# Gated mix of a cached attention and a gated MLP, one token: weights loaded once for several matmuls, the gated unit in rows, and projections added up in two banks

## The chip, the cores and the metric

The kernel runs on one NeuronCore of one Trainium2 chip. A core has a matrix engine (TensorE, PE in the profile; its weight loads are PEld), a vector engine (VectorE, DVE), an activation engine (ScalarE, ACT), GpSimd (POOL) and a queue engine (SyncE, SP) that here issues all large transfers. On-chip memory is SBUF (128 partitions) and PSUM (8 banks of 128 x 512 fp32 into which TensorE writes). Data comes from HBM through 16 DMA engines. The metric is the device time in microseconds (us). The kernel before takes 386.67 us, the median of 7 runs (386.39 to 387.09).

## What is computed

One token `x` of 1024 numbers goes through an attention block A and a mixer block B, mixed by a scalar gate:

```python
g = sigmoid((x * gate_w).sum())
# A: 32 query heads, 4 key/value heads, 65536 cached positions, head size 128
q = x @ wq                                 # 1024 -> 32 x 128
p = softmax(q k^T / sqrt(128));  o = p v   # 8 query heads share one k, v
a = o.reshape(4096) @ wo                   # 4096 -> 1024
# B: F = 3584, Fh = 1792, sequence of one
z = gelu(x_b @ w_in)                       # 1024 -> 3584
z1, z2 = z[:Fh], layernorm(z[Fh:])
b = (z1 * (w_sp * z2 + b_sp)) @ w_out      # 1792 -> 1024
out = g * a + (1 - g) * b
```

In the kernel both blocks read the same `x`. All inputs are bf16. K and V are 64 MiB each, and with the weights 162 MB are read for 2 KB of output.

## The kernel before

Every operation is recorded by `P(engine, function, r=..., w=...)` in program order. A planner derives the waits from what each operation reads and writes; each engine then executes its own operations strictly in the recorded order. So the order in the source is the order on each engine, and whatever is recorded behind a waiting operation on the same engine waits as well.

All large loads go through SyncE into a ring of five slots (`NS = 5`) of 4 MB. The stream is a fixed list: two loads of wq, then K pairs (8192 positions a piece, two pieces a load) mixed with two loads of w_in and one of w_out, then K and V pairs in turn, then wo in pieces. Load n takes the slot of load n - 5, and is issued when the last operation that reads that slot has been recorded as done (`done`, `issue`). Counted from 0, the first loads are: 0 and 1 wq, 2 K 0,1, 3 w_in, 4 K 2,3, 5 w_in, 6 K 4,5, 7 w_out, 8 K 6,7, 9 K 8,9, 10 V 0,1, 11 K 10,11, 12 V 2,3, 13 K 12,13. Load 12 so takes the slot of w_out, and load 11 that of K 4,5.

Query projection (L414 to L442): for each of 8 chunks of x, eight matmuls of 512 columns, spread over four column groups of the array (`tile_position=(0, 32 * cg)`), all into one bank; then a cast, transposes and a selection bring q into a padded form.

K pieces (`k_piece`, L456): a piece is worked in four batches. VectorE transposes 128 x 1024 32-bit words (L464), TensorE runs four matmuls of 512 columns with a weight load each (L472), into one of two score banks; two bank numbers alternate by piece. `score_piece` copies a finished bank to SBUF and takes its maximum. Exponentials lag by one head group (8 pieces); `pt_piece` transposes them and `pv_piece` (L510) multiplies them with V in four column groups (L516). `out_piece` closes a head group: sum, reciprocal, scale, selection, and a column vector `ovec`.

Mixer: `win_piece` (L552) makes the 3584 numbers of z as columns: 28 columns of 128 values, each from matmuls with a moving operand of one column (L558, 224 in all). `mixer_piece` (L566) computes gelu, layernorm and gate on tiles of 128 x 28 and leaves `yb`. `wout_piece` (L599) multiplies by w_out with four column groups of 256 columns (L606) into one bank, which ScalarE copies to `brow`. These pieces are recorded behind K pieces 1, 3 and 6, before the first V arrives.

The end: for each wo load, matmuls of 256 columns in four column groups add into one bank (L650); VectorE adds `brow` (L656) and SyncE writes the output.

## Time and profile before

| what | value |
|---|---|
| time, median of 7 runs | 386.67 us (386.39 to 387.09) |
| the profiled execution | 386.39 us, span in the profile 384.6 us |
| TensorE busy | 230.1 us (60%), 1547 matmuls and 1547 weight loads |
| VectorE busy | 211.7 us (55%) |
| ScalarE busy | 30.6 us (8%) |
| DMA | 162.24 MB, mean 422 GB/s |
| mean granted TensorE clock | 0.798 |

The page divides the span into 40 slices; a digit is a busy share in tenths. A row of a timeline or of the groups names start and length, the engine, the source line (L464 is line 464 of the kernel before), the operation, the tiles it writes and reads, their shape, and in brackets how long the engine had been idle and what ended the idle time. `SPq` rows are the transfers that SyncE issues. The tensor names are only `arena` (all of SBUF), `pb` (the PSUM banks) and the inputs. A row of a stretch ends with the granted TensorE clock, the share of the DMA engines that is busy, and GB/s.

### The profile page before, as it was taken

The page shows a single profiled execution, that of the slowest core. Times are in us where ns is not written, and L with a number is a line of the kernel's source. Part 1 is how long each engine was busy: PE and PEld are TensorE (multiplying, and loading weights), DVE is VectorE, ACT ScalarE, POOL GpSimd, SP SyncE. Part 2 cuts the span into 40 slices and gives each one's busy share as a digit, 9 for nine tenths or more (in the row PEclk, how much of TensorE's full clock was granted, in tenths as well). Part 3 has the DMA queues.
Part 4 walks back from the last instruction along what each step waited for, and adds up shares of the span by engine and source line. Part 5 has one row for each costly group of instructions (what it writes and reads, how often), then busy time and mean ns, then how long its engine had stood idle before and what let it go on. Part 6 is the DMA issues. An engine that isn't in the chain of part 4 may idle for free.

```text
span 384.6 us, 3607 instructions
## 1 busy us (share of the span) xinstructions
PE 230.1 (60%) x1547; PEld 85.0 (22%) x1547; DVE 211.7 (55%) x329; ACT 30.6 (8%) x71; POOL 2.1 (1%) x9
## 2 busy tenths in 40 slices
PE   0444888578766656573686484726873939543334
PEld 0111544523211111121222121212220202211121
DVE  4116464399967474655695656645964748511010
ACT  1000000100300000001010000000100000320000
POOL 2000000000000000000000000000000000000000
PEclk9999959579996969595889596968895869755665
DMA  8999999999999999999999999999999999999994
GB/s 328 436 436 440 431 424 444 422 432 429 428 436 429 421 433 436 433 434 431 433 433 424 433 429 429 429 431 437 429 431 429 436 427 429 428 433 436 409 426 177
DMA packets 6228, 162.24 MB, mean 422 GB/s; under 512 B 700, under 2 KB 708, under 8 KB 964
## 3 DMA queue, kind: packets, MB, share of 16 engines
q1 hardware_dynamic: 6200, 162.01, 98.2%
q8 instruction: 12, 0.20, 0.2%
q14 instruction: 4, 0.03, 0.0%
q10 hardware_dynamic: 12, 0.00, 0.0%
HBM read 162.01 MB, written 0.00 MB: 421 GB/s over the span
## 4 chain that ended last, share of the span: by engine, by line
DMA 72%; PE 15%; DVE 12%; issue 0%; SPq 0%
DMA arena<-in_A_k_cache_dram 59%; PE pb L472 10%; DMA arena<-in_A_v_cache_dram 10%; DVE arena L464 9%; DMA arena<-in_A_wo_dram 3%; PE pb L516 2%; PE pb L558 2%; DVE arena L485 1%; DVE arena L507 0%; PE pb L650 0%; DVE arena L533 0%; PE pb L538 0%; SPq L349 0%; PE pb L528 0%; PE pb L495 0%
## 5 line engine op out<-in xcount | busy, mean ns | idle before, releaser
L472 PE MATMUL pb<-arena 128*128 128x512 bf16 x512 | 156.9, 448 | 96.0 <-DVE arena L464 93.9
L464 DVE STREAM_TRANSPOSE arena<-arena 128x1024 f32<-128x1024 f32 x128 | 151.6, 1217 | 77.3 <-DMA arena<-in_A_k_cache_dram 76.7
L472 PEld LDWEIGHTS pb<-arena 128*128 128x128 bf16 x512 | 45.8, 107 | 202.1 <-DVE arena L464 148.3
L516 PE MATMUL pb<-arena 128*32 128x512 bf16 x512 | 39.3, 442 | 20.4 <-DMA arena<-in_A_v_cache_dram 17.9
L502 ACT ACTIVATE arena<-arena 128x512 bf16<-128x512 f32 x32 | 23.0, 720 | 224.0 <-DVE arena L507 171.2
L507 DVE STREAM_TRANSPOSE arena<-arena 128x512 bf16<-128x512 bf16 x32 | 21.7, 679 | 18.2 <-PE pb L516 18.2
L485 DVE TENSOR_SCALAR_CACHE_REDUCE arena<-pb 128x512 f32<-128x512 f32 x32 | 21.5, 672 | 6.6 <-PE pb L472 6.4
L516 PEld LDWEIGHTS pb<-arena 128*32 128x32 bf16 x512 | 12.8, 106 | 44.3 <-issue 36.2
L558 PEld LDWEIGHTS pb<-arena 128*128 128x128 bf16 x224 | 13.8, 159 | 0.4
L558 PE MATMUL pb<-arena 128*128 128x1 bf16 x224 | 13.7, 198 | 0.0
L650 PE MATMUL pb<-arena 128*1 128x256 bf16 x128 | 7.0, 375 | 7.6 <-DMA arena<-in_A_wo_dram 7.5
L530 DVE RECIPROCAL arena<-pb 128x1 f32<-128x1 f32 x4 | 0.7, 168 | 17.0 <-PE pb L528 17.0
L419 PE MATMUL pb<-arena 128*2 128x512 bf16 x64 | 7.2, 627 | 4.3 <-DMA arena<-in_A_wq_dram 4.3
L656 DVE TENSOR_TENSOR arena<-pb,arena 97x256 bf16<-97x256 f32 x1 | 0.4, 425 | 13.8 <-PE pb L650 13.8
L426 DVE CAST arena<-pb 98x512 bf16<-98x512 f32 x1 | 0.7, 691 | 10.7 <-PE pb L419 10.7
L396 PE MATMUL pb<-arena 1*128 1x2 bf16 x1 | 0.2, 159 | 10.3 <-DMA arena<-in_B_b_sp_dram 10.3
L502 ACT ACTIVATION_READ_ACCUMULATOR arena<-arena 128x1 f32 x32 | 6.0, 186 | 0.0
L650 PEld LDWEIGHTS pb<-arena 128*1 128x1 bf16 x128 | 3.1, 101 | 11.1 <-DMA arena<-in_A_wo_dram 8.7
L538 PE MATMUL pb<-arena 128*128 128x128 bf16 x16 | 1.8, 243 | 5.2 <-DVE arena L533 5.2
L573 ACT ACTIVATE arena<-arena 128x28 f32<-128x28 f32 x1 | 0.2, 227 | 57.0 <-DVE arena L572 57.0
L569 DVE COPY arena<-pb 128x28 f32<-128x28 f32 x1 | 0.2, 188 | 7.8 <-PE pb L558 7.8
L398 DVE COPY arena<-pb 128x2 f32<-128x2 f32 x1 | 0.2, 159 | 7.4 <-PE pb L396 7.4
(88 smaller groups left out, 50.4 us busy)
## 6 DMA issues: line engine op xcount, KB each, us to landing
arena<-in_A_k_cache_dram SPq DMA_DIRECT2D x16, 4096.0 KB, 30.9
arena<-in_A_v_cache_dram SPq DMA_DIRECT2D x16, 4096.0 KB, 36.1
arena<-in_A_wq_dram SPq DMA_DIRECT2D x2, 4096.0 KB, 17.0
arena<-in_B_w_in_dram SPq DMA_DIRECT2D x2, 3584.0 KB, 40.8
arena<-in_A_wo_dram SPq DMA_DIRECT2D x3, 2048.0 KB, 34.5
arena<-in_B_w_out_dram SPq DMA_DIRECT2D x1, 3584.0 KB, 35.0
arena<-in_A_wo_dram SPq DMA_DIRECT2D x1, 1024.0 KB, 23.3
arena<-in_A_wo_dram SPq DMA_DIRECT2D x2, 512.0 KB, 13.8
```

The costliest lines, as they stand in the source:

```text
L419: ins = e.matmul(pf(OB)[32 * cg:32 * cg + 2, :], xw[:, 3 * c + 1 - s:3 * c + 3 - s], sl[:, WQ_N * k + 512 * (4 * s + cg):WQ_N * k + 512 * ...
L426: P("DVE", lambda e: e.tensor_copy(qsb[0:98, :], pf(OB)[0:98, :]), w=[("psb", 0), B(OB)])
L464: P("DVE", lambda e: e.transpose(ktb(i).bitcast(F32), sl[:, 2048 * j:2048 * (j + 1)].bitcast(F32)), r=[key], w=[("kt", i % NKTS)])
L472: ins = e.matmul(pf(sb), qpad[g % 2][:, o:o + 128], vw(ktb(i), 64 * f2 + ev, [[128, 16], [2, 32]]), start=(j == 0 and fe == 0), stop=(j == ...
L485: P("DVE", lambda e: e.tensor_scalar(scs(n), pf(sb), 0.0, None, op0=ALU.add, op1=ALU.max, accum_out=maxc[:, n:n + 1]), w=[("sc", n % NSC), ...
L502: P("ACT", lambda e: e.activation(psb(n), scs(n), ACTF.Exp, bias=gcol(g, K_NB), scale=SCALE, accum_out=lp[:, n:n + 1]), r=[("sc", n % NSC) ...
L507: P("DVE", lambda e: e.transpose(ptsb(n), psb(n)), r=[("psb", n % 2)], w=[("ptsb", n % 2)])
L516: ins = e.matmul(pf(OB)[32 * cg:32 * (cg + 1), :], ptsb(n)[:, 32 * b:32 * (b + 1)], vw(sl, 128 * b, [[2048, 4], [1, 128]]), start=(u == 0 ...
L530: P("DVE", lambda e: e.reciprocal(gcol(g, K_RL), pf(MB)[:, 0:1]), w=[("rl", g), B(MB)])
L538: ins = e.matmul(pf(MB)[:, 0:128], sel[:, 128 * c:128 * (c + 1)], osc[:, 128 * c:128 * (c + 1)], start=(c == 0), stop=(c == 3))
L558: ins = e.matmul(pf(MB)[:, z:z + 1], vw(sl, c0, [[FC, 128]]), xT[:, 2 * i + k:2 * i + k + 1], start=(i == 0 and k == 0 and z == 0), stop=( ...
L650: ins = e.matmul(pf(FB)[32 * q:32 * q + 1, 0:QW], ovec[:, 8 * i + c:8 * i + c + 1], sl[:, o:o + QW], start=(i == 0 and c == 0), stop=(i == ...
```

## The change

Six parts:

- A matmul can be recorded without a weight load (`again`): it uses the weights of the matmul before it. K pieces are worked in pairs: two transposes, then for each of four weights two matmuls into two banks. There are four score banks (1 to 4), four transposed buffers (`NKTS = 4`) and eight score buffers (`NSC = 8`). Both scores of a pair are copied after the first batch of the next pair.
- The query projection uses one column of x as weights for four matmuls into four banks, in two column groups instead of four (`times`), followed by four casts and eight transposes.
- w_in is done the same way, with 448 columns a matmul, so that z lies in rows: 4 partitions (0, 32, 64, 96) of 896 values. The elementwise work of the gated unit runs on 97 x 896 or 97 x 448 instead of 128 x 28 or 128 x 14; the square moves to ScalarE. 14 transposes and eight small copies make `yb`.
- w_out and the first three wo loads are multiplied as rows of 512 columns, two matmuls per weight, without column groups, and add up in banks 0 and 5. Four copies (`keep`) bring the sum to `brow`.
- The first wo load is worked before the last head group's `out_piece`, since `ovec` of the first group is long there.
- The last wo load (three pieces) keeps its form and has its own bank.

The list of loads and their order stay. The program has 1318 matmuls instead of 1536, and 390 of them load no weights.

## Prediction, made before the changed kernel had run

> **What bounds the kernel now.** I read the page first, then SyncE's own queue, the chain of waits, the timelines of TensorE and VectorE around the gated unit, and last the stretches at the end.

> The page: the transfers fill the span.

> ```profile
> span 384.6 us, 3607 instructions
> ...
> DMA  8999999999999999999999999999999999999994
> GB/s 328 436 436 440 431 424 444 422 432 429 428 436 429 421 433 436 433 434 431 433 433 424 433 429 429 429 431 437 429 431 429 436 427 429 428 433 436 409 426 177
> ...
> q1 hardware_dynamic: 6200, 162.01, 98.2%
> q8 instruction: 12, 0.20, 0.2%
> ```

> Only the first and last slices fall short. The change moves no byte of data, so its time can differ in three ways: the transfers run dry, the work behind the last byte changes, or the small share that is not data (12 instruction packets) changes. How far from dry is it? SyncE issues a 4 MB load when a ring slot comes free:

> ```profile
> 71.27 0.33 SPq L349 DMA_DIRECT2D arena<-in_A_v_cache_dram  x1
> 88.22 0.33 SPq L349 DMA_DIRECT2D arena<-in_A_k_cache_dram  x1
> 96.31 0.33 SPq L349 DMA_DIRECT2D arena<-in_A_v_cache_dram  x1
> 98.81 0.33 SPq L349 DMA_DIRECT2D arena<-in_A_k_cache_dram  x1
> ```

> The chain of waits tells when the last of these landed, and so when each had its turn:

> ```profile
> 98.81 38.46 DMA arena<-in_A_k_cache_dram
> ...
> 137.30 1.25 DVE arena L464
> ```

> 137.27 and the chain's next K landing (176.17, four loads later) give 9.73 us a load. Counting from 0, the load issued at 88.22 is load 11, the one at 96.31 load 12. Load 13 lands at 137.27, so load 12's turn begins at 117.8 and load 11's at 108.1 on the latest of the 16 DMA engines, about 2.1 us earlier on the foremost (the engines' own landing marks: 115.7 to 117.8). From issue to the first byte it takes about 2 us: the first three loads (29.1 us) were issued from 0.73 on and the third landed at 32.5, less 0.6 us between engines. So load 12 may be issued at 113.7 at the latest without loss, 17.4 us after 96.31, and load 11 at 104.0, 15.8 us after 88.22. That is all the cover there is. Load 12 waits for the slot of w_out, that is, for the w_out matmuls, which wait for the gated unit.

> TensorE and VectorE there:

> ```profile
> 14.92 3.58 PE L419 MATMUL pb<-arena 128*2 128x512 bf16 x32
> ...
> 64.41 6.83 PE L558 MATMUL pb<-arena 128*128 128x1 bf16 x112
> ...
> 89.59 1.04 PE L472 MATMUL pb<-arena 128*128 128x512 bf16 x4 [0.30 <-DVE arena L464]
> ```

> ```profile
> 71.27 0.19 DVE L569 COPY arena<-pb 128x28 f32<-128x28 f32 x1 [7.81 <-PE pb L558]
> ...
> 72.63 0.33 DVE L575 RECIPROCAL arena<-arena 128x28 f32<-128x28 f32 x1
> ...
> 76.01 0.16 DVE L588 RECIPROCAL arena<-arena 128x1 f32<-128x1 f32 x1 [0.27 <-ACT arena L587]
> ...
> 77.39 1.24 DVE L464 STREAM_TRANSPOSE arena<-arena 128x1024 f32<-128x1024 f32 x1
> ```

> The first row is 32 matmuls in 8 rounds of four column groups, 0.43 us a round: half clock. The K row is four matmuls 0.218 us apart at full clock, each with its own weight load, whose 98 ns are hidden. The gated unit holds VectorE for 6.12 us (71.27 to 77.39), with the K transposes queued behind it.

> The end:

> ```profile
> 376.51 1.87 PE L650 MATMUL pb<-arena 128*1 128x256 bf16 x32 [3.02 <-DMA arena<-in_A_wo_dram]
> ...
> 378.00:379.00 1.00, 0.38 (x8) 0.00 (x0) 0.00 (x0) 0.00 (x0) 0.00 (x0) 0.50 0.59 242
> 379.00:380.00 1.00, 0.93 (x16) 0.41 (x16) 0.00 (x0) 0.00 (x0) 0.00 (x0) 0.50 0.50 193
> 380.00:381.00 1.00, 0.69 (x12) 0.10 (x8) 0.00 (x0) 0.00 (x0) 0.00 (x0) 0.50 0.22 90
> 381.00:382.00 1.00, 0.53 (x8) 0.10 (x8) 0.00 (x0) 0.00 (x0) 0.00 (x0) 0.50 0.00 0
> ```

> The DMA share (second number from the right) falls in steps: the engines finish between 378.3 and 381.4. They drift apart because an instruction packet occupies one engine for about 1.03 us (0.2% of 16 x 384.6, over 12), and some have served two. TensorE does its 32 matmuls of a w_o load in 1.9 us at half clock and idles 3 us.

> **The change part by part.**

> *Weight reuse in K.* 256 of 512 weight loads go. The K row says they were hidden: 0 us. [...]

> *Query projection.* 16 rounds become 64 matmuls of 512 columns, in runs of four on one column group. If the last of a run overlaps the first of the next group, that is 48 rounds, if not 64. From 14.92, some 5 us at half clock (the K run at 33.84 changed after 4 us), the rest at 0.218: done at 28 to 31, before 26.5. Four casts at 0.69 (one before) and the 2.2 us from cast to first transpose: K starts at 33 to 36 instead of 32.5.

> *K pair, w_in.* Eight transposes at 1.16 plus the last matmuls: K done 46 to 50. Each w_in load is 32 matmuls of 448 columns, 0.191 each, 24 or 32 deep: 4.6 to 6.1 us in place of 6.83. K 2,3 lands at 51.8 as before; 9.3 of transposes, 1.3 of scores, 1.8 of matmuls end at 64.2, w_in at 69 to 70.3. The gated unit so begins 1 to 2 us earlier than 71.27.

> *Gated unit in rows.* The same steps run on 97 x 896 instead of 128 x 28. From the nearest rows: four PSUM copies of 448 (0.69 for 512) 2.5; Square and Exp on ScalarE (0.72 for 512) 1.2 each; two tensor_scalars 0.62 each if they go like the f32 cast (0.43 for 512), 1.1 if not; two tensor_tensors (0.67 for 512) 1.1 each. The reciprocal: 0.328 for 28 and 0.164 for 1 give 6.07 ns an element, 5.6 us for 896, the largest item; its bounds are 1.1 (the rate of the other operations) and 10.5 (0.328/28 with no fixed part), and I take the slope because it alone holds for both rows. Reductions, subtract, square, scale on 448 columns 0.4 to 0.6 each, 3.2 together; the two mean/variance hops as before 2.8; 14 transposes 1.4, eight copies at 0.18 1.45. With handoffs 23.4 us, 6.1 before; bounds 18.9 and 29.3, from those of the reciprocal and the tensor_scalars. [...]

> VectorE returns to K 4,5 at 69.7 + 23.4 = 93.1 instead of 77.39. It was 10.8 us from there to load 11's issue, plus about 1 where TensorE restarts cold: 105, limit 104.0 on the foremost engine and 106.1 on the last: no loss that counts. Then the first half of K 6,7 (4.65 + 1.3 + 1.8) to 113, and w_out.

> *w_out and w_o.* w_out was 14 rounds of 256, 1.7 us; now 28 matmuls of 512 in series at 0.218, 6.1 us, 12 at half clock; I take 6.5. Load 12 is issued at 119.5 to 120, limit 113.7. It flows from 121.7. A foremost engine stood ready at 115.7 and needed 262.6 us from there (378.3); all now restart together, and four later instruction packets instead of seven cost 1.2 on the latest: 121.7 + 262.6 + 1.2 = 385.5, against 381.4. **+4.1.**

> *Fewer instructions.* TensorE goes from 3094 matmuls and weight loads to 2268, at 258 to a packet 8 or 9 packets for 12. Without a stall this alone takes one packet off the latest engine, -1.0; here it is in the 1.2.

> *Tail.* Three w_o loads become 16 matmuls of 512 each in series: 3.5 us at full, 6.8 at half clock, against 4.9 between landings. The first stands ahead of the last head group's output chain (2.0 us). Counting back from the landings, full clock from the first on ends at -0.2; half clock throughout would add 9, but every dense run of 512-column matmuls longer than 5.2 us ended at full clock in this trace, which leaves up to +2.7. The four new copies (about 0.38 each, from 0.29 for 128 columns and 0.42 for the final 256-column add) finish 1.7 after the third load, just about with the last piece. I take +0.3.

> Sum: 386.39 (the profiled execution, span 384.6 and 1.8 around it) + 4.1 + 0.3 = 390.8; the median of the runs shown is 0.28 above that execution: **391.1**.

> **Rivals.**

> *The cover is enough.* If the unit takes under 18 us or the matmuls overlap more, w_out is done by 114 and nothing runs dry. For it: the small rows say little of the rate at 896 columns. Against it: it takes 6 us off my sum. Then 386.67 - 1.0 + 0.3 = 386.0, 385.4 to 387.2: the other side. Decides at issue of load 12 before about 114.

> *Twice starved.* Column groups in series, a reciprocal nearer its upper bound, half clock at each restart: load 11 is late too, w_out ends near 125 and 121.7 grows to 127: 396, 394 to 398. For it: each piece follows idle time of TensorE, and it was at half clock from 70 to 80.

> *The w_o chain at half clock.* It loses the 2.7 of the bound instead of 0.3 where the granted clock falls back before the second load: 393.5 with the stall, 388.4 without.

> *No weight is spared on the path* is no rival but the base: the K part counts nothing in any case.

> **How the numbers follow.** Starved once, as summed, 0.60: 388.0 to 394. Cover enough, 0.15. Twice starved, 0.16. Clock in the tail, 0.09. A measurement here tells about 0.2%, 0.77 us. Of the 0.15, 0.07 lies under 385.9 and 0.08 within the bound; the rest is slower, 0.85. The range leaves out about a tenth on each side: 386.8 to 395.3.

> **What would show it.** VectorE's stretch from the PSUM copies to the next K transpose: 23 us, with a reciprocal of 5.6. Load 12 issued near 119.5, a dip of 3 to 5 us in the GB/s slices near 120, none after. 8 or 9 instruction packets. K matmuls still 0.218 apart. The last w_o landing near 385.5 and about 3.2 us behind it. I am wrong if no slice dips, if the dip is twice as deep, or if the time past the last landing grows.

## The result and the profile after

| | before | changed |
|---|---|---|
| time, median | 386.65 us (39 runs, 386.38 to 387.09) | 388.4 us (16 runs, 385.93 to 390.15) |
| the profiled execution | 386.39 us, span 384.6 | 388.5 us, span 386.6 |

The changed kernel is slower: ratio 1.0044, 95% interval 1.0036 to 1.0053. That is 1.75 us, where 4.4 were forecast. The direction and the mechanism of the prediction hold; the size is off by more than a factor of two.

The page of the changed kernel, with the same lines as before: the span, the share of the DMA engines and the GB/s in 40 slices of 9.67 us, and the queues.

```profile
span 386.6 us, 2806 instructions
...
DMA  8999999999999999999999999999999999999993
GB/s 326 434 434 441 426 431 433 434 434 434 434 388 386 434 434 432 434 434 428 432 424 431 434 434 432 434 434 428 434 432 431 434 428 432 431 432 424 415 422 152
...
q1 hardware_dynamic: 6200, 162.01, 97.8%
q8 instruction: 9, 0.15, 0.2%
```

Two slices dip, 388 and 386, on either side of 116 us. Against 432 they lack 90 GB/s together, which is 2.0 us of full flow (90 x 9.67 / 432). The forecast was a dip of 3 to 5 us near 120. Nothing else dips. The row of digits does not show it at all. The busy share is still 9 tenths there.

SyncE's queue (start, length, source line, what is loaded) shows the loads around the dip; in their order they are load 11, 12 and 13:

```profile
101.54 0.33 SPq L358 DMA_DIRECT2D arena<-in_A_k_cache_dram  x1
115.38 0.33 SPq L358 DMA_DIRECT2D arena<-in_A_v_cache_dram  x1
115.75 0.43 SPq L358 DMA_DIRECT2D arena<-in_A_k_cache_dram  x1
```

Load 12 is issued at 115.38, 1.7 us past the limit of 113.7 that the prediction worked out, but 4.4 us sooner than the 119.5 to 120 it forecast. The timeline of VectorE (start, length, operation, shape, in brackets the idle time before and what ended it) shows where those 4.4 us were gained:

```profile
32.59 4.62 DVE L484 STREAM_TRANSPOSE arena<-arena 128x1024 f32<-128x1024 f32 x4 [0.54 <-DMA arena<-in_A_k_cache_dram]
...
51.98 2.37 DVE L484 STREAM_TRANSPOSE arena<-arena 128x1024 f32<-128x1024 f32 x2 [8.37 <-DMA arena<-in_A_k_cache_dram]
...
67.58 2.51 DVE L589 COPY arena<-pb 33x448 f32<-33x448 f32 x4 [5.21 <-PE pb L248]
...
74.53 5.75 DVE L597 RECIPROCAL arena<-arena 97x896 f32<-97x896 f32 x1
...
89.34 0.95 DVE L632 COPY arena<-pb 32x7 bf16<-32x7 bf16 x8 [1.45 <-PE pb L626]
90.30 2.37 DVE L484 STREAM_TRANSPOSE arena<-arena 128x1024 f32<-128x1024 f32 x2
```

K starts at 32.59, as before. The gated unit runs from 67.58 (the first PSUM copy) to 90.30 (the next K transpose), 22.72 us with a reciprocal of 5.75. Its start, not its length, is what came out well ahead of the forecast (69.7). TensorE's timeline says why, with a stretch of the query projection and one of w_in:

```profile
22.91 0.39 PE L429 MATMUL pb<-arena 128*1 128x512 bf16 x2 [1.86 <-DMA arena<-in_A_wq_dram]
23.12 0.82 PE L248 MATMUL pb<-arena 128*1 128x512 bf16 x6
23.77 0.39 PE L429 MATMUL pb<-arena 128*1 128x512 bf16 x2
...
64.26 0.36 PE L429 MATMUL pb<-arena 128*1 128x448 bf16 x2
64.45 0.74 PE L248 MATMUL pb<-arena 128*1 128x448 bf16 x6
65.02 0.36 PE L429 MATMUL pb<-arena 128*1 128x448 bf16 x2
```

L429 is the matmul with a weight load, L248 the one without (in `again`). Each group counts two of the first and six of the second: one run on each column group. The next two start 0.86 us later (512 columns) and 0.76 us later (448). Eight matmuls so pass in the time of four: K's matmuls of 512 columns start 0.218 us apart, four of them in 0.87. The program issues four on one column group and then four on the other, and still both runs go side by side.

The end of the span. First the stretches of 1 us (length, busy time and count of PE, weight loads, DVE, ACT, POOL; then the granted clock, the DMA share and GB/s), then the timeline:

```profile
380.00:381.00 1.00, 1.00 (x6) 0.17 (x2) 0.00 (x0) 0.00 (x0) 0.00 (x0) 1.00 0.53 217
381.00:382.00 1.00, 1.00 (x16) 0.29 (x12) 0.00 (x0) 0.00 (x0) 0.00 (x0) 1.00 0.20 74
382.00:383.00 1.00, 1.00 (x24) 0.53 (x26) 0.60 (x2) 0.00 (x0) 0.00 (x0) 1.00 0.02 8
```

```profile
381.97 1.38 PE L704 MATMUL pb<-arena 128*1 128x256 bf16 x26
382.38 1.70 DVE L655 COPY arena<-pb 1x256 f32<-1x256 f32 x4 [6.29 <-PE pb L248]
384.12 0.42 DVE L710 TENSOR_TENSOR arena<-pb,arena 97x256 bf16<-97x256 f32 x1
```

Each of the 16 DMA engines marks in the trace when its part of a load has landed. These landing marks put the end of the last load at 379.8 on the foremost engine and at 382.9 on the latest; before it was 378.3 and 381.4. So +1.5 us on both. The final add starts at 384.12, 1.2 us behind the last landing (before 0.7: 382.12 behind 381.4). TensorE ends at 383.35; the four copies end at 384.08, and the add waits for them. Together 1.5 + 0.5 = 2.0 us, which is the whole difference of the spans.

### The profile page after: what moved, and what is told of

The parts are those of the page before. It is cut to its first block, busy times and chain, and to the rows that moved or that the text cites. A ratio compares the mean times of both kernels' runs of the same rounds, so it can differ in the third digit from the quotient of the medians.

```text
span 386.6 us, 2806 instructions
## 1 busy us (share of the span) xinstructions
PE 230.8 (60%) x1329; PEld 53.7 (14%) x939; DVE 230.6 (60%) x350; ACT 31.8 (8%) x71; POOL 3.8 (1%) x11
## 3 DMA queue, kind: packets, MB, share of 16 engines
q1 hardware_dynamic: 6200, 162.01, 97.8%
HBM read 162.01 MB, written 0.00 MB: 419 GB/s over the span
## 4 chain that ended last, share of the span: by engine, by line
DMA 49%; DVE 28%; PE 21%; issue 1%; ACT 1%; SPq 0%; DVEq 0%
DMA arena<-in_A_k_cache_dram 40%; DVE arena L484 17%; DMA arena<-in_A_wo_dram 9%; PE pb L248 8%; PE pb L494 6%; DVE arena L507 3%; PE pb L641 2%; PE pb L538 2%; DVE arena L529 2%; DVE arena L597 1%; DVE arena L589 1%; SPq L358 0%; DVE arena L557 0%; DVE arena L655 0%; PE pb L626 0%
## 5 line engine op out<-in xcount | busy, mean ns | idle before, releaser
L484 DVE STREAM_TRANSPOSE arena<-arena 128x1024 f32<-128x1024 f32 x128 | 148.8, 1211 | 62.9 <-DMA arena<-in_A_k_cache_dram 53.1
L494 PE MATMUL pb<-arena 128*128 128x512 bf16 x256 | 114.9, 449 | 87.8 <-DVE arena L484 81.1
L248 PE MATMUL pb<-arena 128*128 128x512 bf16 (+2 forms) x390 | 143.0, 430 | 0.0
L494 PEld LDWEIGHTS pb<-arena 128*128 128x128 bf16 x256 | 27.6, 108 | 198.0 <-DVE arena L484 113.5
L538 PE MATMUL pb<-arena 128*32 128x512 bf16 x512 | 40.5, 452 | 18.8 <-DMA arena<-in_A_v_cache_dram 15.8
L641 PE MATMUL pb<-arena 128*1 128x512 bf16 x38 | 15.4, 404 | 1.2 <-DMA arena<-in_A_wo_dram 1.2
L442 DVE CAST arena<-pb 33x512 bf16<-33x512 f32 x4 | 2.7, 683 | 11.1 <-PE pb L248 11.0
L429 PE MATMUL pb<-arena 128*1 128x512 bf16 (+1 forms) x32 | 6.7, 410 | 2.2 <-DMA arena<-in_A_wq_dram 1.9
L597 DVE RECIPROCAL arena<-arena 97x896 f32<-97x896 f32 x1 | 5.8, 5753 | 0.0
L589 DVE COPY arena<-pb 33x448 f32<-33x448 f32 x4 | 2.5, 617 | 5.2 <-PE pb L248 5.2
L655 DVE COPY arena<-pb 1x256 f32<-1x256 f32 x4 | 1.7, 416 | 6.3 <-PE pb L248 6.3
```

The source lines that it names most:

```text
L248: return e.add_instruction(mybir.InstMatmult(start_tensor_calc=start, stop_tensor_calc=stop, tile_size=m.tile_size, tile_position=m.tile_p ...
L429: ins = e.matmul(out, xT[:, c:c + 1], sl[:, o:o + n], start=(c == 0), stop=(c == KC - 1), tile_position=(0, 32 * cg), skip_group_check=True)
L442: P("DVE", lambda e, b=b: e.tensor_copy(vw(qsb, 512 * (b // 2), [[1, 512]], 64 * (b % 2), 33), pf(SCB[b])[0:33, :]), w=[("psb", 0), ("psb" ...
L484: P("DVE", lambda e, m=m, sl=sl: e.transpose(ktb(i + m).bitcast(F32), sl[:, 2048 * j:2048 * (j + 1)].bitcast(F32)), r=[key], w=[("kt", (i ...
L494: ins = e.matmul(pf(sb[0]), qpad[g % 2][:, o:o + 128], rhs[0], start=st, stop=sp)
L538: ins = e.matmul(pf(OB)[32 * cg:32 * (cg + 1), :], ptsb(n)[:, 32 * b:32 * (b + 1)], vw(sl, 128 * b, [[2048, 4], [1, 128]]), start=(u == 0 ...
```

## The experiments

The theory: VectorE's longer gated unit and the longer w_out issue load 12 late, and the transfers run dry. The rivals: the loss lies behind the last landing; the instruction packets or the changed K pieces account for it.

**One cheap operation in place of the reciprocal** (`no_reciprocal`): the kernel leaves out the division in gelu.

```diff
-        P("DVE", lambda e: e.reciprocal(u, u), r=KT_, w=KT_)
+        P("DVE", lambda e: e.tensor_scalar(u, u, 1.0, None, op0=ALU.add), r=KT_, w=KT_)
```

> The changed kernel with the 97x896 reciprocal of the gated unit (5.75 us) replaced by one more tensor_scalar (0.63): leaves out the division in gelu. Theory 1, late w_out: load 12 (V 2,3) goes out 5.1 us sooner, at about 110.3, under the limit of 113.7, so nothing runs dry; the last landing falls from 382.9 to about 380.5 (foremost engine 378.3 again, 2.2 of drift), the dip in the GB/s slices near 120 goes, and the time is 385.9 (-2.5). Its runs lie within 1 us of each other, where those of the changed kernel spread over 4. Theory 2, the end of the kernel: the 2 us come from the w_o rows and the four copies; the unit hides behind transfers and 388.4 stays (387.9 to 388.9).

Measured: 386.65 us (385.92 to 387.18, 10 runs), ratio 0.9998, interval 0.9988 to 1.0007. SyncE's queue:

```profile
109.89 0.33 SPq L358 DMA_DIRECT2D arena<-in_A_v_cache_dram  x1
```

Load 12 goes out 5.5 us sooner, ahead of the limit, no slice of GB/s dips, and the last load lands from 378.3 to 381.2, as before the change. With VectorE 5.1 us shorter the kernel gives back 1.75 us, all that it had lost. So the loss hangs on the gated unit, through load 12. The remaining parts of the change cost and bring nothing that the median shows. The expected 385.9 and the 1 us of spread were missed: the latest engine still lands at 381.2, and the ten times lie in two groups, 385.92 to 386.32 and 386.98 to 387.18.

**The reciprocal three times** (`three_reciprocals`).

```diff
         P("DVE", lambda e: e.reciprocal(u, u), r=KT_, w=KT_)
+        P("DVE", lambda e: e.reciprocal(u, u), r=KT_, w=KT_)
+        P("DVE", lambda e: e.reciprocal(u, u), r=KT_, w=KT_)
```

> The changed kernel with the reciprocal done three times over (1/x, x, 1/x): 11.5 us more on VectorE, same output. Theory 1: load 12 goes out at about 126.9, and since every DMA engine stands dry there, all of it shows: 399.9 (398.5 to 400.5). Theory 2: under 1 us more, 388.4 to 389.4.

Measured: 399.62 us (398.39 to 400.27, 4 runs), ratio 1.0331, interval 1.0311 to 1.0351. SyncE's queue, and the GB/s of the page:

```profile
126.26 0.33 SPq L358 DMA_DIRECT2D arena<-in_A_v_cache_dram  x1
```

```profile
GB/s 334 450 433 423 419 433 445 441 426 423 271 225 253 423 443 453 425 421 423 433 441 436 433 423 421 433 443 437 423 431 424 426 440 431 426 436 430 415 426 187
```

Two more reciprocals are 11.5 us, and the time grows by 11.2 over the changed kernel (399.62 less 388.4; the two profiled executions, 398.39 and 388.5, differ by 9.9, and load 12 goes out 10.9 later in them). Past the limit, a microsecond on VectorE was about a microsecond of the kernel here. Now three slices dip (271, 225, 253), and the last load lands from 390.8 to 392.9. No rival accounts for this: nothing at the end was touched, and there are 9 instruction packets as in the changed kernel.

**w_out sooner** (`wout_sooner`): the w_out pieces are recorded one K piece earlier, so that load 12 goes out sooner while all the work stays.

```diff
             load([("wout", 0), ("wout", 1)], [(0, rows(B_w_out, 0, 14))])
-        elif n == 6:
             aux = (("wout", 0), ("wout", 1))
```

> The changed kernel with the w_out matmuls recorded behind K piece 5 instead of 6; the loads and their order stay. Theory 1: w_out starts when K 4,5 is done, about 101.5, and ends near 108, so load 12 goes out 5.7 under the limit and nothing is dry: 385.9, runs within 1 us. K 6,7 waits about 6 us on TensorE, which its load's successor (load 13, due near 127) does not feel. Theory 2: 388.4, as w_out is the same length.

Measured: 386.58 us (386.07 to 387.31, 10 runs), ratio 0.9998, interval 0.9988 to 1.0007. SyncE's queue, then the timeline of the end:

```profile
102.01 0.33 SPq L357 DMA_DIRECT2D arena<-in_A_k_cache_dram  x1
110.11 0.33 SPq L357 DMA_DIRECT2D arena<-in_A_v_cache_dram  x1
```

```profile
380.89 1.25 PE L703 MATMUL pb<-arena 128*1 128x256 bf16 x26
...
381.31 1.70 DVE L654 COPY arena<-pb 1x256 f32<-1x256 f32 x4 [6.29 <-PE pb L248]
...
383.04 0.42 DVE L709 TENSOR_TENSOR arena<-pb,arena 97x256 bf16<-97x256 f32 x1
```

Moving one line in the order takes the loss away with all the arithmetic in place. Load 11 goes out at the same time as in the changed kernel (102.01, 101.54), so load 11 wasn't what cost it. The last load lands from 378.3 to 381.3, but the add comes 1.7 us later, again behind the copies. The ten times lie in two groups, 386.07 to 386.34 and 386.81 to 387.31; the profiled execution is of the upper one. In it the first w_o load was worked at half clock up to 370.8 (the granted clock is 0.50 from 366 to 369 and 0.70 from 369 to 372). In the profile of `no_reciprocal` (386.01 us, of its lower group) the clock was full in that work (1.00 from 366 on) and the add came at 381.70. That the clock there makes the two groups fits these two profiles; no others were kept.

**w_in on one column group** (`win_one_group`): both runs of four go to column group 0, and so into the same rows; half of z is not formed, the number of matmuls and weight loads stays.

```diff
+    def times(e, i, sl, width, n, banks, at, one=False):
...
+                    g = 0 if one else 32 * cg
-                    out = pf(banks[b])[32 * cg:32 * cg + 1, 0:n]
+                    out = pf(banks[b])[g:g + 1, 0:n]
...
-                                       tile_position=(0, 32 * cg), skip_group_check=True)
+                                       tile_position=(0, g), skip_group_check=True)
...
+        P("PE", lambda e: times(e, i, sl, F, FZ, ZB, lambda b, cg: FH * (b // 2) + FZ * (2 * (b % 2) + cg), True),
```

> The changed kernel with both runs of four w_in matmuls on the same column group (half of z then adds into the wrong rows). If the two groups ran at the same time in the changed kernel, as the 32 matmuls in 2.9 us say, each w_in load now takes 6.1 us, twice. Theory 1: the first of the two costs nothing (VectorE waits 8.4 us for K 2,3 anyway, until 51.98), the second moves the gated unit and load 12 by 2.9 to 3.2 us: 391.4 (390.8 to 392). Theory 2: 388.4. If the groups had not overlapped: no change in the w_in rows at all.

Measured: 390.76 us (390.22 to 392.82, 4 runs), ratio 1.0115, interval 1.0088 to 1.0143. TensorE in the first w_in load and at the start of the second, then VectorE, then SyncE's queue:

```profile
44.90 0.35 PE L430 MATMUL pb<-arena 128*1 128x448 bf16 x1
45.09 0.73 PE L248 MATMUL pb<-arena 128*1 128x448 bf16 x3
45.65 0.35 PE L430 MATMUL pb<-arena 128*1 128x448 bf16 x1
...
65.63 0.35 PE L430 MATMUL pb<-arena 128*1 128x448 bf16 x1
```

```profile
71.95 2.51 DVE L590 COPY arena<-pb 33x448 f32<-33x448 f32 x4 [8.22 <-PE pb L248]
```

```profile
119.97 0.33 SPq L358 DMA_DIRECT2D arena<-in_A_v_cache_dram  x1
```

Now a run of four takes the 0.75 us in which eight went before. In this profile the gated unit starts at 71.95 (67.58), 4.4 us later where 2.9 to 3.2 were expected: the second w_in load takes 6.2 us instead of 3.2, and it starts 1.4 later (65.63, 64.26), since TensorE worked K 2,3 at half clock up to 62.1 instead of 57.3 (the page has 8 tenths of granted clock in the slice from 58.6 on, that of the changed kernel 9 in the slice from 58.0 on). Load 12 is issued at 119.97. That is the issue that the prediction summed (119.5 to 120), but 1.4 us of it came from the clock, and this execution took 392.82, the longest of the four. The median of 390.76 is near the 391.1 forecast, but when load 12 was issued in the other executions is not known. Only the second w_in load counts. After the first one VectorE still waits for K 2,3, until 51.81.

**w_out and w_o in their old form** (`old_projections`): 256 columns in four column groups, one bank each, no copies at the end; K, the query projection and the gated unit stay as changed.

```diff
-    def project(e, vec, sl, first, last):
...
+            for c in range(7):
+                for q in range(4):
+                    ins = e.matmul(pf(MB)[32 * q:32 * q + 1, 0:QW], yb[:, 7 * i + c:7 * i + c + 1],
...
-    wo_piece(1)
-    wo_piece(2)
-    keep()
-    for i, c0, c1 in WO[3:]:
+    for i, c0, c1 in WO:
```

> The changed kernel with w_out and w_o as in the kernel before (256 columns, four column groups, one bank; no four copies, no early w_o). Late w_out: it takes 1.7 us instead of 6.2, load 12 goes out at about 110.8, under 113.7, nothing runs dry. The end is the old one, 0.7 us from last landing to the add, whatever the granted clock. 2460 instructions of TensorE, 9 or 10 packets. Time 386.2 (385.8 to 386.6), runs within 0.8 of each other. If it were the row form of the gated unit or of q that costs, 388.4 stays.

Measured: 386.60 us (386.34 to 386.89, 11 runs; before 386.59 beside it), ratio 1.0, interval 0.9991 to 1.0009. w_out in TensorE's timeline, then SyncE's queue:

```profile
109.41 1.70 PE L640 MATMUL pb<-arena 128*1 128x256 bf16 x56
```

```profile
111.15 0.33 SPq L358 DMA_DIRECT2D arena<-in_A_v_cache_dram  x1
```

w_out takes 1.70 us instead of the 6.2 it takes in rows (109.14 to 115.3), load 12 goes out at 111.15, and the loss is gone. So the rows of w_out and the gated unit in rows are late only together: w_out in its cheap form suffices, and so do 5.1 us off the gated unit. Most of the instructions that the change removes are gone here too (2458 matmuls and weight loads for 3094, 9 packets for 12), and this gains nothing; the last load lands at 381.7 on the latest engine.

**The K pairs alone** (`k_pairs_alone`): the kernel before with only K worked in pairs and weights used twice.

```diff
-    NKTS = 3
-    NSC = 10
+    NKTS = 4
+    NSC = 8
-    SCB = [3, 4]
+    SCB = [1, 2, 3, 4]
...
-                ins = e.matmul(pf(sb), qpad[g % 2][:, o:o + 128], vw(ktb(i), 64 * f2 + ev, [[128, 16], [2, 32]]),
-                               start=(j == 0 and fe == 0), stop=(j == 3 and fe == 3))
+                ins = e.matmul(pf(sb[0]), qpad[g % 2][:, o:o + 128], rhs[0], start=st, stop=sp)
+                ins = again(e, ins, pf(sb[1]), rhs[1], st, sp)
```

> The kernel before with the K pieces alone in pairs, each loaded weight serving two matmuls. If weight loads are hidden: K matmuls stay 0.218 us apart at full clock, and only a packet of instructions goes (256 weight loads): 386.5 (386.1 to 386.8). If a weight load costs time between matmuls: batches of eight in less than 1.75 us at full clock, though the transfers still set the end.

Measured: 386.71 us (386.40 to 386.96, 11 runs), ratio 1.0002, interval 0.9993 to 1.001. TensorE in a K pair:

```profile
89.00 0.38 PE L246 MATMUL pb<-arena 128*128 128x512 bf16 x1
89.22 0.38 PE L485 MATMUL pb<-arena 128*128 128x512 bf16 x1
89.43 0.38 PE L246 MATMUL pb<-arena 128*128 128x512 bf16 x1
89.65 0.38 PE L485 MATMUL pb<-arena 128*128 128x512 bf16 x1
```

With a weight load (L485) or without (L246), the matmuls start 0.21 to 0.22 us apart, as they did before with a load each. The reuse that gives the change its name is worth nothing here: 256 weight loads go, and no microsecond.

**More instructions** (`more_matmuls`): the kernel before, with 32 matmuls of one column added behind each of 28 V pieces, into a bank that nothing reads. They run where TensorE idles, and bring instruction packets.

```diff
+        def more(e):
+            for b in range(32):
+                ins = e.matmul(pf(1)[:, 0:1], idb, xT[:, 0:1], start=True, stop=True)
+            return ins
+        if n < 28:
+            P("PE", more, r=["idb", "xT"], w=[B(1)])
```

> The kernel before with 32 more one-column matmuls, weight loads included, behind each of the first 28 V pieces: 1792 more instructions for TensorE, 1.9 us of its time a piece, no data moved. If instruction packets hold up the DMA engine that carries them: 19 packets instead of 12, the latest engine serves one more (1.1 to 1.6 us), the last landing is at 382.5 to 383.0 and the time 387.8 (387.2 to 388.6). If they cost nothing: 386.65.

Measured: 388.10 us (387.92 to 388.35, 4 runs), ratio 1.0039, interval 1.0025 to 1.0053. The page, and the stretches at the end:

```profile
q8 instruction: 19, 0.31, 0.3%
```

```profile
379.00:380.00 1.00, 0.92 (x20) 0.27 (x8) 0.00 (x0) 0.00 (x0) 0.00 (x0) 0.50 0.55 225
380.00:381.00 1.00, 0.41 (x12) 0.29 (x16) 0.00 (x0) 0.00 (x0) 0.00 (x0) 0.50 0.55 225
381.00:382.00 1.00, 0.86 (x20) 0.21 (x12) 0.00 (x0) 0.00 (x0) 0.00 (x0) 0.50 0.19 66
```

Seven packets more cost 1.5 us. The DMA share stands at 0.55 for two whole stretches: nine of sixteen engines are still at work (9/16 = 0.56). The landing marks have seven engines between 378.3 and 378.9, and nine between 381.2 and 382.9.

**Both mended** (`sooner_and_split`): w_out sooner, and two of the four copies at the end go to ScalarE.

```diff
-        elif n == 6:
             aux = (("wout", 0), ("wout", 1))
...
+            if b == WB0:
+                P("DVE", lambda e, q=q, src=src: e.tensor_copy(brow[32 * q:32 * q + 1, :], src),
+                  r=[B(b)], w=[("brow", q)])
+            else:
+                P("ACT", lambda e, q=q, src=src: e.activation(brow[32 * q:32 * q + 1, :], src, ACTF.Copy),
+                  r=[B(b)], w=[("brow", q)])
```

> The changed kernel with w_out behind K piece 5, and the four copies of the end shared: two on VectorE, two on ScalarE. Nothing dry. In the run with w_out behind K piece 5 alone the copies ended 0.9 us behind TensorE (383.01 against 382.14) where the granted clock was half in the first w_o load, and the runs lay at 386.1 to 386.3 or at 386.8 to 387.3. If the copies set that: the upper runs fall by about 0.8, median 386.2. If TensorE's rows set it: 386.6 as without the split.

Measured: 386.20 us (385.99 to 386.57, 11 runs; before 386.59), ratio 0.999, interval 0.9981 to 0.9999. The timeline of the end:

```profile
379.92 0.84 DVE L656 COPY arena<-pb 1x256 f32<-1x256 f32 x2 [7.07 <-PE pb L248]
379.92 0.76 ACT L659 ACTIVATE arena<-pb 1x256 f32<-1x256 f32 x2 [32.68 <-PE pb L248]
...
381.75 0.42 DVE L713 TENSOR_TENSOR arena<-pb,arena 97x256 bf16<-97x256 f32 x1 [0.98 <-PE pb L707]
```

The copies take 0.84 us in place of 1.70, the add now waits for TensorE, and the upper group of times is gone (no run above 386.57). The times show this, not the profile: in it the clock was full in the first w_o load (9 tenths or more in the slices from 365 on), where the copies ended together with TensorE in `no_reciprocal` too. This version is faster than the changed kernel by 2.2 us, and than the kernel before by 0.1%, with an interval that just excludes no difference.

The profiled executions of these kernels line up by the issue of load 12:

| kernel | load 12 issued | past 113.7 | last load, foremost engine | latest engine |
|---|---|---|---|---|
| before | 96.31 | - | 378.3 | 381.4 |
| `no_reciprocal` | 109.89 | - | 378.3 | 381.2 |
| `old_projections` | 111.15 | - | 378.3 | 381.7 |
| changed | 115.38 | 1.7 | 379.8 (+1.5) | 382.9 (+1.5) |
| `win_one_group` | 119.97 | 6.3 | 384.5 (+6.2) | 386.7 (+5.3) |
| `three_reciprocals` | 126.26 | 12.6 | 390.8 (+12.5) | 392.9 (+11.5) |

The loss on the foremost engine is the time past 113.7, to 0.2 us, at three points. The limit that the prediction took from the trace of before is the right one.

## Why the prediction was right in direction and wrong in size

| step | forecast | measured |
|---|---|---|
| weight reuse in K | 0 | 0 (`k_pairs_alone`, ratio 1.0002) |
| query projection | 48 to 64 rounds, done 28 to 31 | 32 rounds, done 26.5 |
| K starts | 33 to 36 | 32.59 |
| a w_in load | 4.6 to 6.1 us | 3.2 us (64.26 to 67.46) |
| gated unit starts | 69.7 | 67.58 |
| gated unit | 23.4 us, reciprocal 5.6 | 22.72 us, reciprocal 5.75 |
| load 11 issued | 105 | 101.54 |
| w_out | 6.5 us | 6.2 us |
| load 12 issued | 119.5 to 120 | 115.38 |
| last landing, latest engine | +4.1 | +1.5 |
| behind it | +0.3 | +0.5 |

**The step that failed** is the sentence "If the last of a run overlaps the first of the next group, that is 48 rounds, if not 64", and with it the 24 or 32 rounds of a w_in load. The two column groups overlap entirely: 32 rounds, and 16 for w_in. That moves the start of the gated unit by 2.1 us. The other 2.3 of the 4.4 us are small errors of one sign: the gated unit 0.7, K 4,5 behind it 0.7, the half of K 6,7 and w_out 0.9. `win_one_group` tests the step by itself: without the overlap a w_in load takes 6.2 us instead of 3.2, and the median rises by 2.4 (390.76 less 388.4). The trace of before had the evidence only in part: it showed four column groups side by side when every matmul changes the group (32 matmuls in 8 rounds of 0.43 us), not when four in a row use the same one. The "about 1 where TensorE restarts cold" is an estimate that no run shows by itself: from the end of the unit to the issue of load 11 it was 11.24 us (90.30 to 101.54), against 10.83 before, with K 4,5 at a granted clock of 0.50 from 92.7 to 98.

**A second term was wrong in the other direction.** The prediction let all engines restart together, so that only 1.2 us of later packets would part the foremost from the latest, against 3.1 before. By its own sum, with the measured issue, the last landing would have been 115.38 + 2.0 + 262.6 + 1.2 = 381.2, and the change would have cost nothing at the end. Measured are 382.9. The foremost engine came out as summed (380.0 summed, 379.8 measured); the spread at the end stayed at 3.1 us. The engines did not restart together: load 11 lands from 115.7 to 117.7, load 12 from 127.0 to 130.2. The last landing marks of the sixteen engines lie 1.3 to 1.9 us later at every rank than in `no_reciprocal`: the late engines lost about as much as the early ones, although the latest still had data up to 117.7 and so, by the same 2 us, a limit of 115.7. Why it lost time stays open. With deeper stalls the spread shrinks to 2.2 and 2.1 us, not to 1.2. The two errors, 4.4 us too late and 1.7 us too close together, leave 2.6 of the 4.1 us.

**"Without a stall fewer packets alone: -1.0"** fell too. With 9 packets for 12 and no stall the latest engine ends at 381.2 (`no_reciprocal`), 381.3 (`wout_sooner`) and 381.7 (`old_projections`), against 381.4. In `no_reciprocal` all but one engine have landed by 380.2, where four landed at 381.4 before; its last instruction packet runs from 380.0 to 381.1. That fits one late packet holding the last engine, however many came earlier. So the rival "the cover is enough" was no gain but a draw, as the three kernels show that are this case: 386.65, 386.58 and 386.60, against 386.0 in the prediction.

**The tail** was sized about right for a reason that was half right. The copies take 0.42 us each (0.38 forecast), but they finish 0.7 us after the last piece in the profile, not with it. Where the first w_o load was worked at full clock they are hidden (`no_reciprocal`). The time past the last landing grew from 0.7 to 1.2, which the prediction named as a sign of being wrong, although its own sum had +0.3 there.

**The other rivals.** "Twice starved" is what `three_reciprocals` brings about: load 11 at 112.42, 399.62 us. Between the two, `win_one_group` issues load 11 at 106.13, past its own limit of 104.0, and still loses on the foremost engine only what load 12 is late: load 11 lands 1.9 later than before, load 12 6.2. "The w_o chain at half clock" came in part: in the profile of `wout_sooner` the add stood 1.7 us behind the last landing, against 0.7 before: a microsecond, not the 2.7 of the bound. Its 388.4 without a stall equals the measured median by chance: the profile shows the stall, and only 0.5 us more behind the last landing.

**What held:** that the slack ahead of load 12 decides, and that it would be overrun; the limit of 113.7; the reciprocal by the slope of two rows (5.6 forecast, 5.75 measured); K's weight loads hidden behind its matmuls (0.21 to 0.22 us a matmul with a load or without). The limit held as a sum, but its 2 us are not all a wait for the first byte: in the changed kernel the first packet begins 0.95 us after the issue of load 12, and the rest is a slow first packet (last section). "Half clock" in the query projection is a pace of 0.43 us a round: the profile of before grants 1.00 from 12 to 25 us and has no 0.50 before 48.0. From there on K's matmuls in a batch start 0.43 us apart where it grants 0.50, and 0.22 where it grants 1.00.

**What stays open:** the runs of the changed kernel spread over 4.2 us, those of before over 0.7. The time past the limit may depend on how soon TensorE reaches full clock ahead of w_out (in the profiled execution the granted clock is 0.50 from 77 to 97 us, and half clock lasts to about 98), and every microsecond past the limit counts. That fits, as the kernels whose load 12 is in time spread over 0.5 to 1.3 us, and as half clock cost w_in 1.4 us in the profile of `win_one_group`. But the other executions left no trace, so it is argued, not shown.

## What to carry to other kernels

In a kernel that the transfers fill, ask of an edit by how much it moves the issue of the loads that wait for it, against the slack that the trace gives, and what it adds behind the last landing; up to the limit the first cost nothing here, past it about a microsecond for each. Where an edit overruns that slack, look first at the order: recording w_out one piece sooner gave back everything, with no work removed. And saving work (weight loads, instructions) on an engine that waits anyway is not a gain; here it brought nothing (ratios 1.0002 and 1.0 in `k_pairs_alone` and `old_projections`), while 1.7 us of late issue cost 1.5 of the 2.0 us that the profiles differ by.

## What was not expected of the hardware

- Two column groups ran side by side although each got four matmuls in a row. The first matmul of the second group starts 8 ns behind the first of the first group (22.906 and 22.914 us), ahead of three matmuls that the program has before it. So the strict order on each engine, as the section on the kernel before has it, did not hold here for the starts of matmuls of another column group.
- Instruction packets of 16 KB (0.20 MB in 12) went over the same DMA engines as the data, 0.93 to 1.11 us each in the profiles of before and changed, and by the landing marks only over nine of the sixteen: in `more_matmuls`, with 19 packets, the other seven are done by 378.9, as with 9 (379.1 in `no_reciprocal`). Seven more cost 1.5 us; three fewer brought 0.2 at most.
- After the transfers had run dry the first packet of most engines took 1.6 to 2.2 us, where a packet takes 1.21 in the flow; the first one began 0.95 us after the issue. The start of the kernel before is alike (issue at 0.73, first packet at 1.75, first packets of 1.6 to 2.2 us).
